# Order of the weight loads, of two norms and of the first projections at the start of an attention and gated-unit kernel

## The chip, the cores and the metric

The kernel runs on one core of a Trainium2 chip. The time is device microseconds of one execution; the text quotes medians of several executions. A profile is one execution taken by the hardware profiler, and its span (first to last instruction) is about 2 us shorter than the time. The engines are TensorE (PE in the profile; PEld is its weight load), VectorE (DVE), ScalarE (ACT), GpSimd (POOL) and SyncE (SP). SP and ACT also issue the loads. PEclk is the granted TensorE clock.

Some executions take 2 to 4 us longer, with a mean granted clock of 0.994 or less instead of 0.996 to 1.000. The ratios and intervals below count most of them as fast runs, because they lie within 1.5% of the fastest. Beside each ratio I therefore give the difference of the medians of the runs at a mean clock of 0.996 or more, called "full-clock runs". The kernel before differed from itself by 0.22 us in that measure; a smaller difference is not resolved here.

## The reference, cut to what matters

```python
B, S, D, F = 1, 2048, 512, 1792          # bfloat16
xn = layernorm(x)                        # no gain or bias, eps 1e-5
def A(xn):                               # sliding-window attention
    q, k, v = split_heads(xn @ wqkv)     # 32 heads of 16; wqkv is 512 x 1536: queries, keys, values
    p = softmax(mask(q @ k.T / 4))       # causal, window 256
    return (p @ v) @ wo
def B(xn):                               # gated unit without an activation
    return ((xn @ w_gate) * (xn @ w_up)) @ w_down
out = x + A(xn) + B(xn)
```

The change is aimed at the first 21 us. In that time the kernel loads x and the weights, normalises the first 512 rows of x (four blocks of 128 rows), transposes them on TensorE, and computes their queries, keys and values.

## The kernel before

The program is static, but its order is not written by hand. While the kernel is built, a small list scheduler works through the operations with assumed durations and assumed landing times of the loads, and emits each instruction to its engine in the order that this gives. On the chip the engines took their lists in this order, each instruction waiting for its data. The numbers `land`, `wkv` and `wq` are such assumptions: they change no wait, only the order. Below, values 0, keys 0 and queries 0 are the projections of block 0 of x; Wv, Wk and Wq are the three thirds of Wqkv; a load has landed when its last byte is there; and an apply is the instruction that normalises a block. The mode switches of the prediction are changes between groups of matmuls (dense, values, scores), for which the scheduler assumes a cost.

```python
def prologue(self):
    load(nc.sync,   self.x[0:64, 0, :],   xv[0:64, 0, :])        # block 0, two halves on two queues
    load(nc.scalar, self.x[64:128, 0, :], xv[64:128, 0, :])
    load(nc.scalar, self.x[:, 1, :],      xv[:, 1, :])           # block 1
    for k, cols in ((0, slice(512, 1536)), (2, slice(512, 1536))):   # keys AND values, in two halves
        load(nc.sync, self.Wqkv[:, k:k + 2, cols], w["qkv"][:, k:k + 2, cols])   # of the contraction
    load(nc.sync, self.x[:, 2, :], xv[:, 2, :])
    load(nc.sync, self.Wqkv[:, :, 0:512], w["qkv"][:, :, 0:512]) # queries
    load(nc.sync, self.x[:, 3, :], xv[:, 3, :])
    # ... cut: gate, up, down and output weights, the rest of x, constants
    self.keep_busy(42, 0)                # matmuls on ones, to warm up TensorE

def first_chunk(self):
    land = (3.6, 3.9, 7.3, 8.8)          # assumed landing of the four blocks of x
    wkv, wq = 6.3, 8.4                   # assumed landing of the weights
    applied, roots = [], []
    for b in range(4):
        # ... cut: bn = bn_stats + bn_aggr on DVE
        s = self.op(f"st{b}", {"V": ...}, [land[b]] + applied * (b == 1), bn, rank=0.5)
        s = self.op(f"sq{b}", {"A": ...}, [s], ...)     # sqrt(var + eps) on ACT
        s = self.op(f"rs{b}", {"V": ...}, [s], ...)     # reciprocal on DVE
        # ... cut: ap{b} on DVE, (x - mean) * rs; block 0 in two halves
        if b == 0:
            applied = [self.at_["ap", 0, 1]]            # block 1's statistics wait for block 0's apply
    for b in range(4):
        # ... cut: turn{b}: 4 transposes on PE, then a copy PSUM -> xnT by ACT or DVE
        self.add_v(0, b, wkv - 0.6)                                  # 16 matmuls each
        self.add(f"k0b{b}", 4.2, [("xnT", 0, b), wkv], ..., k_out)   # inner loop over k = 0..3
        self.add(f"q0b{b}", 4.2, [("xnT", 0, b), wq], ..., q_out)

def add_v(self, T, b, land=0.0):         # values: OUTER loop over k, so half the weights do half the work
    def emit(i):
        for k in range(4):
            for jj in range(2):
                # ... cut: 2 matmuls, lhsT = xnT[:, k, 64 tokens], rhs = Wqkv[:, k, 1024:1536]
```

The softmax here doesn't subtract the row's maximum and nothing guards it: scores larger than these inputs give would overflow.

## Time and profile before

| | before |
|---|---|
| time, median of 5 runs | 267.28 us (267.13 to 267.55) |
| time and span of the profiled run | 267.0 us, 265.0 us |
| PE busy | 259.0 us, 98% of the span |
| first value projection starts | 6.03 us |
| PE without a gap from | 9.46 us |

The chain of work that ended last, in order of time, starts like this (start us, length us, what; L148 is the loading helper, L205 the dense matmuls, L679 the value projections, L614 the transposes, L213 the scores):

```profile
3.32 6.10 DMA Wqkv<-in_A_wqkv_dram
9.41 0.05 issue
9.46 2.85 PE M L205 x48
...
20.03 0.33 PE S L213 x8
20.36 0.99 PE M L679 x16
```

After that the chain stays on PE until 258.9 us. So the kernel is bound by PE from 9.46 us on, and by loads before. The busy time by stretch, kernel before (each group: busy us and number of instructions; then PEclk, DMA share, GB/s):

```profile
5.00:9.46 4.46, 3.24 (x45) 2.40 (x45) 3.13 (x9) 2.04 (x6) 0.00 (x0) 1.00 1.04 366
9.46:20.00 10.54, 10.54 (x164) 9.11 (x168) 9.64 (x20) 4.51 (x8) 3.07 (x12) 1.00 1.07 378
20.00:260.00 240.00, 240.00 (x3202) 115.12 (x3202) 173.47 (x329) 156.62 (x106) 115.75 (x251) 1.00 0.11 29
```

From 9.46 to 260 us PE is busy all the time (10.54 of 10.54, 240.00 of 240.00); only the first line has something to win. What happens in it, from the timeline of the kernel before (start us, length us, engine, line, operation, out<-in, shapes, count, and in brackets the idle time before it and what ended that):

```profile
3.39 0.69 DVE L584 BATCH_NORM_STATS2 st<-x 128x6 f32<-128x512 bf16 x1 [1.46 <-DMA x<-in_A_x_dram]
4.86 0.60 DVE L271 TENSOR_SCALAR xn<-x,mv,rs 128x256 bf16<-128x256 bf16 x2
5.27 0.54 PE L614 MATMUL M<-ident,xn 128*128 128x128 bf16 x4 [0.63 <-DVE xn L271]
5.38 0.69 DVE L584 BATCH_NORM_STATS2 st<-x 128x6 f32<-128x512 bf16 x1
6.03 0.63 PE L679 MATMUL M<-Wqkv,xnT 128*64 128x256 bf16 x8
7.37 0.63 PE L679 MATMUL M<-Wqkv,xnT 128*64 128x256 bf16 x8 [0.71 <-DMA Wqkv<-in_A_wqkv_dram]
7.93 1.07 PE L205 MATMUL M<-xnT,Wqkv 128*128 128x128 bf16 x16
8.84 0.39 PE L614 MATMUL M<-ident,xn 128*128 128x128 bf16 x4
9.46 2.85 PE L205 MATMUL M<-xnT,Wqkv 128*128 128x128 bf16 x48 [0.24 <-DMA Wqkv<-in_A_wqkv_dram]
```

Values 0 stop half-way for the second half of the key and value weights (7.37). Then come keys 0 and the transposes of block 1, and then PE waits for the query weights (9.46).

### The profile page before, as it was taken

The numbers are of one execution on the slowest core, as the hardware profiler recorded it, in microseconds if no ns is written. First come the engines' busy times: TensorE is split into PE (matmuls) and PEld (weight loads), VectorE is DVE, ScalarE is ACT, GpSimd is POOL, SyncE is SP. The second block draws the span as 40 slices with busy tenths as digits, with TensorE's granted clock in tenths as the row PEclk, the third lists the DMA queues.
The fourth block names the chain that finished last, engine by engine and source line by source line (L and its number), as shares of the span: only waits on it lengthen the run. The fifth ranks groups of instructions, "written<-read, shape, count | busy, mean of one in ns | idle before, by whom it ended". The sixth has DMA issues, their size and how long they took to land.

```text
span 265.0 us, 8000 instructions
## 1 busy us (share of the span) xinstructions
PE 259.0 (98%) x3456; PEld 131.1 (49%) x3456; DVE 189.7 (72%) x367; ACT 165.0 (62%) x122; POOL 119.9 (45%) x272
## 2 busy tenths in 40 slices
PE   7899999999999999999999999999999999999994
PEld 6784444554435444465534454446545444544562
DVE  4889987888997628787997629796754449787404
ACT  4536676667767766777767676667886776673000
POOL 1223765654357372808256463708164545537000
PEclk9999999999999999999999999999999999999999
DMA  6999920000000400000001400000000000000002
GB/s 201 378 377 349 205 43 0 4 0 2 4 2 20 101 22 24 0 2 2 2 0 42 82 21 22 0 6 0 2 2 22 20 24 22 0 2 0 2 2 80
DMA packets 16739, 13.88 MB, mean 52 GB/s; under 512 B 7104, under 2 KB 16192, under 8 KB 16704
## 3 DMA queue, kind: packets, MB, share of 16 engines
q1 hardware_dynamic: 16336, 13.11, 16.5%
q8 instruction: 27, 0.44, 0.7%
q10 hardware_dynamic: 368, 0.26, 0.4%
q14 instruction: 8, 0.07, 0.1%
HBM read 9.70 MB, written 2.10 MB: 45 GB/s over the span
## 4 chain that ended last, share of the span: by engine, by line
PE 94%; DMA 3%; SPq 1%; DVE 1%; issue 0%
PE M L205 72%; PE S L213 9%; PE M L243 7%; PE M L679 5%; DMA Wqkv<-in_A_wqkv_dram 2%; SPq L148 1%; DMA out_dram<-xn 1%; PE S L205 1%; DVE xn L773 1%; PE M L614 0%
## 5 line engine op out<-in xcount | busy, mean ns | idle before, releaser
L495 ACT ACTIVATE P<-S 128x2048 bf16<-128x2048 f32 x76 | 140.9, 1854 | 55.2 <-PE S L213 51.7
L222 POOL TENSOR_SCALAR_AFFINE_SELECT P<-P 64x256 bf16<-64x256 bf16 (+1 forms) x248 | 112.8, 457 | 112.9 <-ACT P L495 100.8
L205 PE MATMUL M<-xnT,Wg 128*128 128x512 bf16 x224 | 57.7, 380 | 0.0
L205 PE MATMUL M<-xnT,Wu 128*128 128x512 bf16 x224 | 57.7, 380 | 0.0
L205 PE MATMUL M<-Wd,hT 128*128 128x512 bf16 (+1 forms) x224 | 52.1, 373 | 0.0
L731 DVE TENSOR_TENSOR hT<-M,gsb 128x512 bf16<-128x512 f32 x56 | 38.0, 678 | 7.6 <-PE M L205 7.3
L205 PEld LDWEIGHTS <-hT 128*128 128x128 bf16 x238 | 21.7, 98 | 23.5 <-issue 2.1
L205 PEld LDWEIGHTS <-Wu 128*128 128x128 bf16 x224 | 20.5, 98 | 25.1 <-issue 2.3
L205 PEld LDWEIGHTS <-Wg 128*128 128x128 bf16 x224 | 20.2, 98 | 24.5 <-issue 2.8
L201 DVE CAST gsb<-M 128x512 bf16<-128x512 f32 x40 | 27.4, 684 | 4.9 <-PE M L205 4.6
L205 PE MATMUL M<-xnT,Wqkv 128*128 128x128 bf16 (+1 forms) x224 | 30.4, 288 | 0.2 <-DMA Wqkv<-in_A_wqkv_dram 0.2
L531 DVE STREAM_TRANSPOSE at<-M 128x512 f32<-128x512 f32 x32 | 21.4, 698 | 12.3 <-PE M L243 12.3
L213 PE MATMUL S<-Q,K 32*128 32x320 bf16 (+3 forms) x720 | 30.0, 254 | 0.0
L228 DVE TENSOR_TENSOR P<-P,masks 128x512 int16<-128x512 int16 x56 | 22.5, 409 | 9.2 <-ACT P L495 9.2
L213 PEld LDWEIGHTS <-K 32*128 32x128 bf16 x720 | 11.9, 92 | 32.3 <-issue 31.3
L282 DVE TENSOR_SCALAR K<-M,own 128x512 bf16<-128x512 f32 x28 | 20.0, 743 | 3.7 <-PE M L205 3.4
L205 PEld LDWEIGHTS <-Wqkv 128*128 128x128 bf16 x224 | 15.8, 98 | 11.1 <-issue 1.4
L243 PE MATMUL M<-P,V 64*17 64x320 bf16 (+4 forms) x1440 | 19.5, 252 | 0.0
L773 DVE TENSOR_TENSOR y<-M,x 128x512 bf16<-128x512 f32 x12 | 8.2, 682 | 14.6 <-PE M L205 14.6
L243 PEld LDWEIGHTS <-V 64*17 64x17 bf16 x1440 | 17.1, 86 | 2.8 <-issue 0.8
L679 PE MATMUL M<-Wqkv,xnT 128*64 128x256 bf16 x256 | 15.9, 274 | 0.7 <-DMA Wqkv<-in_A_wqkv_dram 0.7
L205 PE MATMUL M<-Wo,OT 128*128 128x512 bf16 (+1 forms) x64 | 16.2, 374 | 0.0
(51 smaller groups left out, 134.0 us busy)
## 6 DMA issues: line engine op xcount, KB each, us to landing
Wg<-in_B_w_gate_dram SPq DMA_DIRECT2D x2, 896.0 KB, 10.3
Wu<-in_B_w_up_dram SPq DMA_DIRECT2D x2, 896.0 KB, 12.1
Wqkv<-in_A_wqkv_dram SPq DMA_DIRECT2D x3, 512.0 KB, 5.0
out_dram<-y SPq DMA_DIRECT2D x12, 128.0 KB, 1.7
x<-in_A_x_dram SPq DMA_DIRECT2D x1, 1024.0 KB, 14.1
Wd<-in_B_w_down_dram SPq DMA_DIRECT2D x2, 512.0 KB, 12.4
Wd<-in_B_w_down_dram SPq DMA_DIRECT2D x2, 384.0 KB, 8.5
x<-in_A_x_dram SPq DMA_DIRECT2D x1, 512.0 KB, 11.6
```

The costliest lines, as they stand in the source:

```text
L201: self.nc.vector.tensor_copy(out=out, in_=in_)
L205: self.nc.tensor.matmul(ps, lhsT=a, rhs=b, start=first and n == 0, stop=last and n == len(pairs) - 1)
L213: self.nc.tensor.matmul(self.S[:, e, 64 * at:64 * (at + m)], lhsT=self.K[U % 3][rows, c, j].rearrange("p l t -> p (l t)"), rhs=self.Q[T % ...
L222: self.nc.gpsimd.affine_select(out=v, in_=v, pattern=[[0, 4], [0, n], [sign, 64]], base=0, fill=0.0, compare_op=ALU.is_gt if kind else ALU ...
L228: self.nc.vector.tensor_tensor(out=v, in0=v, in1=m, op=ALU.bitwise_and)
L243: self.nc.tensor.matmul(banks[lane][32 * e:32 * e + 17, 64 * q:64 * (q + m)], lhsT=self.V[U % 3][rows, j, 4 * c + e, 0:17], rhs=P[rows, e, ...
L282: self.nc.vector.tensor_scalar(out=out, in0=in_, scalar1=own, scalar2=None, op0=ALU.mult)
L495: ex = self.op(f"exp{g}", {"A": (took + 0.06, took + 0.18)}, [o], lambda e: self.nc.scalar.activation(out=P[:, :, 0:hi], in_=self.S[:, :, ...
L531: t = self.op(f"tr{v}", {"V": (0.63, 0.71)}, [o] + ts, lambda e, par=par: nc.vector.transpose(out=self.at[:, :, par, :], in_=self.M[banks[ ...
L679: self.nc.tensor.matmul(self.M[i][64 * lane:64 * lane + 64, 256 * jj:256 * jj + 256], lhsT=self.xnT[T % 2][:, k, tok], rhs=w[:, lane], sta ...
L731: x = self.op(f"u{T}.{f}", {"V": PSUM_COPY["V"]}, [o, ("gate", T, f)], lambda e: self.nc.vector.tensor_tensor(out=self.hT[T % 2][:, f, :], ...
L773: self.nc.vector.tensor_tensor(out=keep["y"][:, cols], in0=self.M[i][:, cols], in1=self.x[:, t, cols], op=ALU.add)
```

## The change

Its intent is to let PE start on values as soon as a third of the weights is there, and to have two blocks ready by then: load values, keys and queries one by one; compute the statistics of block 1 right after those of block 0; tell the scheduler landing times that put both value projections ahead of the keys.

```diff
-        for k, cols in ((0, slice(512, 1536)), (2, slice(512, 1536))):
-            load(nc.sync, self.Wqkv[:, k:k + 2, cols], w["qkv"][:, k:k + 2, cols])
-        load(nc.sync, self.x[:, 2, :], xv[:, 2, :])
-        load(nc.sync, self.Wqkv[:, :, 0:512], w["qkv"][:, :, 0:512])
-        load(nc.sync, self.x[:, 3, :], xv[:, 3, :])
+        for n, lo in enumerate((1024, 512, 0)):
+            load(nc.sync, self.Wqkv[:, :, lo:lo + 512], w["qkv"][:, :, lo:lo + 512])
+            if n:
+                load(nc.sync, self.x[:, n + 1, :], xv[:, n + 1, :])
...
-        land = (3.6, 3.9, 7.3, 8.8)
-        wkv, wq = 6.3, 8.4
+        land = (3.4, 3.9, 8.0, 9.9)
+        wv, wk, wq = 6.2, 7.7, 9.6
...
-            s = self.op(f"st{b}", {"V": (0.92, 0.94)}, [land[b]] + applied * (b == 1), bn, rank=0.5)
+            s = self.op(f"st{b}", {"V": (0.92, 0.94)}, [land[b]], bn, rank=0.5)
...
-            self.add_v(0, b, wkv - 0.6)
-            self.add(f"k0b{b}", 4.2, [("xnT", 0, b), wkv], lambda i, f=project: f(i, 512), k_out)
+            self.add_v(0, b, wv)
+            self.add(f"k0b{b}", 4.2, [("xnT", 0, b), wk], lambda i, f=project: f(i, 512), k_out)
```

The built order on PE becomes: transposes 0, four warming matmuls, transposes 1, values 0, values 1, keys 0, queries 0, transposes 2, keys 1, queries 1, transposes 3, and so on, with values 2 and 3 after the first scores. Before, it was: transposes 0, values 0, keys 0, transposes 1, queries 0, keys 1, queries 1.

More of the change, by code (lines that the diff above doesn't have):

```diff
@@ L573, in first_chunk @@
     def first_chunk(self):
-        land = (3.6, 3.9, 7.3, 8.8)
-        wkv, wq = 6.3, 8.4
+        land = (3.4, 3.9, 8.0, 9.9)
+        wv, wk, wq = 6.2, 7.7, 9.6
         nc = self.nc
-        applied, roots = [], []
+        roots = []
         for b in range(4):
@@ L597, in first_chunk @@
                 self.at_["ap", b, n] = self.op(f"ap{b}", {"V": took}, [s], lambda e, b=b, cols=cols: self.i_apply(b, cols), rank=0)
-            if b == 0:
-                applied = [self.at_["ap", 0, 1]]
         self.op("table", {"A": (1.5, 1.5)}, roots + [("Q", 0, 0, 2)], lambda e: nc.scalar.activation(
```

## The prediction

> **What bounds the kernel now.** TensorE. The page shows PE busy 259.0 us of a 265.0 us span (98%) at a granted clock of 1.0; the chain of waits is 94% PE. Read in order of time, that chain starts with the third Wqkv load (3.32 to 9.41 us), and from 9.46 us runs without a break on PE to 258.9 us. The change moves work but removes none, so it can gain only what PE loses before 9.46 us, plus mode switches.
>
> **The start, from the timeline.** Warm-up matmuls end at 4.64. The first norm (statistics at 3.39, apply at 4.86) lets the transposes start at 5.27 and the first value projection at 6.03. It stops half-way, for 0.71 us, for the second Wqkv half (landed 7.33). Keys run 7.93 to 9.00, transpose 1 at 8.84, then PE waits for Wq (landed 9.41).
>
> **What the change does.** Loads: the same bytes in the same places, so I expect Wv near 5.8, Wk near 7.3, Wq near 9.4 us. Rows of Wv and Wk shrink from 2048 to 1024 B; packets of 1024 B take about 45 ns, of 2048 B 81 to 93 ns: the same rate, which agrees with the Trainium skill, "DMA: Bandwidth & Descriptors", Specifications (line rate from 512 B).
> DVE: statistics of block 1 (x landed 3.75) run directly after those of block 0, so apply 0 starts at about 5.40 instead of 4.86; apply 1 ends near 6.6 instead of 7.26.
> PE order, from the built program: transposes 0, four fillers, transposes 1, values 0 and 1, keys 0, queries 0, transposes 2, keys and queries 1, transposes 3, four projections, first gate and up, first scores, then values 2 and 3 together (before: 1 and 2 together, 0 and 3 alone).
>
> **Sum (estimate from these durations).** Transposes 0 start 5.4 + 0.41 = 5.8 and end 6.35; fillers to 6.74; transposes 1 to 7.13. Values 0 start at 7.1, over a microsecond later than before, but without a stop: values 0 and 1 take 1.87 us (32 matmuls in the chain) to 9.0. Keys 0 to 9.95, then queries 0, 0.5 us after Wq landed. No later wait should appear: apply 2 is ready at 10.5 against its use near 10.9, apply 3 at 12.6 against 13.2.
> From 7.13 the chain's durations give 13.8 us until all projections of block 0, first gate/up and first scores are done: 20.95 us. Before, that point is 21.35. Gain 0.4 us, of which 0.1 us is the pairing of the values (32 take 1.87, twice 16 take 1.98). Everything after is PE-bound and moves left by it; the built program has as many matmuls (3456) and 180 instead of 182 mode stretches.
>
> The clock should stay at 1.0: the longest PE gap is about 1.2 us; the Trainium skill, "TensorE: Matmul & The Clock Gate", Part 1, names some 3.4 us of idling.
>
> **Prediction.** 266.9 us, range 266.3 to 267.5. Faster by over 2%: 0.01; within 2%: 0.98; slower: 0.01.
>
> **What would show it.** Timeline: no DMA wait on PE after 5 us; values 0 start near 7.1; continuous PE from there; first scores near 19.1 instead of 19.96; last value projection ends near 21.0. The chain begins with x loads, DVE and PE rather than Wqkv.
>
> **What would make it wrong.** Wq later than 10 us; block 0's norm delayed over 0.6 us; evacuations (DVE holds apply 2 behind a value copy) stopping PE between 9 and 17 us; new small PE stalls later, since evacuations are reassigned between DVE and ACT.

## The result, and the profile after

| | before | after |
|---|---|---|
| time, median of 5 runs | 267.28 us (267.13 to 267.55) | 266.00 us (265.92 to 266.21) |
| time and span of the profiled run | 267.0 us, 265.0 us | 266.21 us, 264.4 us |
| first value projection starts | 6.03 us | 6.62 us |
| PE without a gap from | 9.46 us | 9.85 us, with three projections done instead of two |
| first scores and all value projections of the first 512 rows done | 21.35 us | 20.65 us |

The ratio is 0.9952, interval 0.9938 to 0.9967. A ratio here is the mean time of one kernel's fast runs over that of the other's of the same rounds, so it is not quite the ratio of the medians quoted. By the 2% measure the two are the same; the gain of 1.28 us is still well outside the scatter of this group, and outside the predicted range (266.3 to 267.5).

The same lines of the timeline, kernel after:

```profile
3.33 0.69 DVE L583 BATCH_NORM_STATS2 st<-x 128x6 f32<-128x512 bf16 x1 [1.39 <-DMA x<-in_A_x_dram]
4.16 0.66 DVE L583 BATCH_NORM_STATS2 st<-x 128x6 f32<-128x512 bf16 x1
5.12 0.60 DVE L270 TENSOR_SCALAR xn<-x,mv,rs 128x256 bf16<-128x256 bf16 x2
5.52 0.54 PE L611 MATMUL M<-ident,xn 128*128 128x128 bf16 x4 [0.41 <-DVE xn L270]
6.30 0.40 PE L611 MATMUL M<-ident,xn 128*128 128x128 bf16 x4
6.62 1.94 PE L676 MATMUL M<-Wqkv,xnT 128*64 128x256 bf16 x32
8.49 1.07 PE L204 MATMUL M<-xnT,Wqkv 128*128 128x128 bf16 x16
9.85 1.07 PE L204 MATMUL M<-xnT,Wqkv 128*128 128x128 bf16 x16 [0.29 <-DMA Wqkv<-in_A_wqkv_dram]
```

The apply of block 0 comes 0.26 us later than before (5.12 against 4.86), not 0.54 as I had it. Values 0 and 1 run as one unbroken stretch of 32 matmuls from 6.62. Keys 0 follow without a wait. Queries 0 still wait, 0.29 us, for the query weights. Those land later than before; the loads of Wqkv, before and after (count, size, median us from issue to landing):

```profile
Wqkv<-in_A_wqkv_dram SPq DMA_DIRECT2D x3, 512.0 KB, 5.0
```

```profile
Wqkv<-in_A_wqkv_dram SPq DMA_DIRECT2D x3, 512.0 KB, 5.6
```

The chain of the kernel after, in order of time:

```profile
3.42 6.39 DMA Wqkv<-in_A_wqkv_dram
9.81 0.05 issue
9.85 1.07 PE M L204 x16
...
18.45 0.33 PE S L212 x8
18.78 1.87 PE M L676 x32
```

So the chain still begins with the query weights, landing at 9.81 instead of 9.41 us. The gain is the third projection that PE has finished by then.

The two profiles differ by 0.59 us of span (264.97 and 264.39 unrounded), the medians by 1.28 us. The sum, from the traces: the start of the last value projection's last matmul moved from 21.08 to 20.38 (0.70 gained); from there to the last matmul the kernel after needs 240.22 us against 240.08 (0.13 lost, told below); the end is equal within 0.01. Outside the span, time minus span is 2.0 us before and 1.8 us after (0.2 gained). The traces show one thing there: behind the last instruction of all five profiles of the order of before, two packets move that the profile calls "instruction" (8 KB each, in the DMA view of the 4 us behind the span), the last of them 1.41 to 1.42 us behind it, once 1.69; in the order of after there are none. In two experiments told below the last one starts 1.32 us behind (e_norms, time minus span 1.93) and 1.13 us behind (e_wqlate, 1.75). Where such packets come, the time outside is longer the later the last one comes (r_before, with 1.69 and 2.00, is the exception); that they cause it was not tested. The rest, 0.49 us, is that the profiled run of before was faster than its five timed runs (267.0 against 267.28) and that of after the slowest of its five (266.21 against 266.00).

### The profile page after: what moved, and what is told of

Same layout as the page of the kernel before. It is cut to its first block, busy times and chain, and to the rows that moved or that the text cites. A ratio compares the mean times of both kernels' runs of the same rounds, so it can differ in the third digit from the quotient of the medians.

```text
span 264.4 us, 7996 instructions
## 1 busy us (share of the span) xinstructions
PE 259.3 (98%) x3456; PEld 131.7 (50%) x3456; DVE 187.2 (71%) x362; ACT 167.6 (63%) x127; POOL 119.9 (45%) x272
## 4 chain that ended last, share of the span: by engine, by line
PE 93%; DMA 3%; SPq 1%; ACT 1%; DVE 1%; issue 0%; ACTq 0%
PE M L204 71%; PE S L212 9%; PE M L242 7%; PE M L676 5%; DMA Wqkv<-in_A_wqkv_dram 2%; SPq L148 1%; ACT P L494 1%; DMA out_dram<-xn 1%; PE S L204 1%; DVE xn L770 1%; PE M L611 0%; ACTq L494 0%
## 5 line engine op out<-in xcount | busy, mean ns | idle before, releaser
L200 DVE CAST gsb<-M 128x512 bf16<-128x512 f32 x38 | 26.0, 683 | 5.8 <-PE M L204 5.7
L281 DVE TENSOR_SCALAR K<-M,own 128x512 bf16<-128x512 f32 x24 | 17.2, 742 | 2.3 <-PE M L204 2.1
L198 ACT ACTIVATE gsb<-M 128x512 bf16<-128x512 f32 x18 | 10.8, 598 | 9.0 <-PE M L204 9.0
```

The source lines that it names most:

```text
L200: self.nc.vector.tensor_copy(out=out, in_=in_)
L281: self.nc.vector.tensor_scalar(out=out, in0=in_, scalar1=own, scalar2=None, op0=ALU.mult)
```

## The experiments

Eighteen runs were made, in five groups, each on one chip and beside its own runs of the kernel before. All gave correct results.

### Repeats of both kernels

No edit. The question was whether the gain is fixed, or set in each run by the loads.

> The kernel before, unchanged, for a second profile and an A-A comparison. Theory A (the whole gain is PE idling saved in the first 21 us; I mis-sized the norm chain of block 0): ratio 1.000 within 0.1%; the point where first scores and the last value projection of block 0 are both done is again near 21.35 us in its trace. Theory B (the first profile of before was a lucky one, and typical runs start PE's unbroken stretch later, because the loads land later or the clock is released later): ratio again 1.000, but this profile shows that point 0.3 us or more later, with the Wq load landing at 9.7 or later.

> The changed kernel, unchanged, for a second profile. Ratio 0.995 (about 1.3 us less). Theory A: first scores and value projections 2 and 3 done at 20.65 us again, and the Wq load lands after 9.8 us again, because its loads have 1024-byte rows. Theory B: that point lies at 20.3 us or earlier, with Wq landing near 9.4, since the first profile was of the slowest of the five runs.

> The changed kernel once more, for a third profile and five more times; two earlier groups gave medians 266.0 (all within 0.3) and 266.9 (266.19 to 270.75). Theory A (a fixed gain): 266.0 to 266.3 again, ratio 0.995. Theory C (the start of the unbroken PE stretch is set in each run by when block 1 of x and Wq land; the floor is 264.1 us of span): the spans of the runs lie between 264.1 and 265.6, and in the profile the span is 244.0 us plus the start of the 64th value-projection matmul of the first chunk, whatever that is.

> The changed kernel a fourth time, as the yardstick of this group. Ratio 0.995 to 0.9985, as its groups so far.

> The changed kernel as the yardstick for the version with both additions on the same chip: 0.5 to 1.0 us faster than before, in the profile a wait of queries 0 for Wq of 0.3 to 0.4 us if Wq lands after 9.8.

| run | median (range), us | ratio to before (interval) | full-clock medians: this, before, difference |
|---|---|---|---|
| first group | 266.00 (265.92 to 266.21) | 0.9952 (0.9938 to 0.9967) | 266.00, 267.28, -1.28 |
| r_before | 267.03 (266.76 to 268.99) | 1.0009 (0.9986 to 1.0032) | 266.94, 267.16, -0.22 |
| r_after | 266.90 (266.19 to 270.75) | 0.9985 (0.9971 to 0.9999) | 266.68, 267.16, -0.48 |
| r_after2 | 266.41 (265.89 to 266.65) | 0.9941 (0.9905 to 0.9977) | 266.41, 267.23, -0.82 |
| r_after3 | 266.58 (266.27 to 266.84) | 0.9971 (0.9948 to 0.9994) | 266.58, 267.16, -0.58 |
| r_after4 | 266.43 (266.15 to 269.69) | 0.9996 (0.9957 to 1.0034) | 266.41, 267.02, -0.61 |

The gain of full-clock runs is 0.5 to 0.8 us in four groups and 1.28 in the first; the kernel after has full-clock medians of 266.4 to 266.7 in those four, inside the range that I predicted. So it is partly the draw of the first group that put the measured time outside that range. Theory A (a fixed gain) falls. Of theory C two parts hold. The spans of the full-clock runs lie between 264.1 and 265.6. And behind the last value projection every profile of one order takes the same time within 0.12 us (240.08 before, 240.22 to 240.33 after), whatever happened ahead of it.

What differs between runs is, first, when x and the weights land: in the full-clock profiles of the kernel after, values 0 start at 6.62 to 7.09 us and the wait for Wq is 0.29 to 0.40 us. A second thing differs, which the mean clock does not show: when the clock is first released. In the profiles where this falls into the warm-up, its matmuls start about 107 ns apart up to the first record of the full clock and 56 to 60 ns apart behind it. That record lies between 3.49 and 6.66 us in all profiles but one. In r_after4 (6.47) the apply of block 0 started at 5.10, as in the first profile (5.12), but from the first transpose to values 0 it took 1.24 us instead of 1.10. So a full-clock run can hide a late release.

The runs of 264.1 us of span are 0.3 us below the first profile, which is what that profile's wait for Wq would account for; no profile was taken of such a run, so this is argued and not shown. Theory B of r_before (a long stretch that starts later, Wq landing at 9.7 or later) failed: Wq landed at 9.20 and the stretch started at 9.24. Its point of first scores and value projections lies at 21.14, not at 21.35 again. The profile of r_after fell on a slow run and decides neither of its two theories.

### The loads alone, the order alone

e_loads and e_loads2 are the kernel before with the load lines of the diff only; the order on every compute engine is exactly that of before. e_oldloads and e_oldloads2 are the kernel after with those lines put back; every compute engine has exactly the order of after.

```diff
 e_loads, against before: only the loads of Wqkv, x block 2 and x block 3 as in the kernel after
 e_oldloads, against after: only these loads as in the kernel before
```

> Before with only the loads changed (values, keys, queries one by one); the instruction order of every compute engine is exactly that of before. Theory A: no gain, ratio 0.999 to 1.002: values 0 no longer stop half-way, but keys 0 then wait for Wk (7.3 to 8.0 us) and queries 0 for Wq (9.4 to 9.8 us), which still begins the unbroken stretch of PE. A rival (the loads themselves are the gain, the data arrive in the order of use): ratio 0.997 or less, unbroken stretch from before 9.3 us.

> The new loads with the order of before, again. If the new loads are a wash or a small loss by themselves: ratio to before 1.000 to 1.002, as in its first group (1.0013). If they gain by themselves: 0.998 or less.

> The changed kernel with only the loads put back as before (two halves of keys and values, then queries); the order on every compute engine is exactly that of the changed kernel. Theory A: most of the gain stays, ratio to before 0.995 to 0.997: values 0 start near 6.6, stop up to 0.6 us for the second half (7.3 us), keys 0 end near 9.7, queries 0 right after. The rival (the loads are the gain): ratio 0.999 or more.

> The changed order with the loads of before, again. If the new loads are a wash (they cure the stop inside values 0 but all landings come some 0.4 us later): within 0.3 us of the changed kernel of this group. If they carry a part of the gain where the chip's landings are favourable: 0.4 us or more slower than the changed kernel.

| run | median, us | ratio (interval) | full-clock difference to before |
|---|---|---|---|
| e_loads | 267.40 | 1.0013 (1.0001 to 1.0025) | +0.24 |
| e_loads2 | 267.48 | 1.0008 (0.9987 to 1.0028) | +0.32 |
| e_oldloads | 266.67 | 0.9994 (0.9967 to 1.0021) | -0.51 |
| e_oldloads2 | 266.51 | 0.9999 (0.9961 to 1.0037) | -0.72 |
| both changes, same two chips (r_after, r_after3) | 266.90 and 266.58 | 0.9985 and 0.9971 | -0.48 and -0.58 |

The two e_oldloads groups hold one and two slow-clock runs (269.12; 269.19 and 268.67), which is why their ratios say nothing; the other runs lie between 266.40 and 266.85. The order carries the gain. The loads by themselves lose a quarter of a microsecond, because PE then waits for each of the three. From the timeline of e_loads:

```profile
6.41 1.06 PE L678 MATMUL M<-Wqkv,xnT 128*64 128x256 bf16 x16 [0.36 <-DMA Wqkv<-in_A_wqkv_dram]
7.91 1.07 PE L204 MATMUL M<-xnT,Wqkv 128*128 128x128 bf16 x16 [0.43 <-DMA Wqkv<-in_A_wqkv_dram]
9.79 2.85 PE L204 MATMUL M<-xnT,Wqkv 128*128 128x128 bf16 x48 [0.59 <-DMA Wqkv<-in_A_wqkv_dram]
```

Under the new order the loads are a wash: full-clock medians of 266.68 with the new loads against 266.65 with the old ones on one chip, 266.58 against 266.43 on the other. They cure the stop inside values 0, and everything lands later: over the profiles with the loads of before the first part of Wqkv landed at 6.0 us on average (5.8 to 6.4) and Wq at 9.5 (six profiles each), with the new loads at 6.6 (6.0 to 7.0) and 9.9 (eight profiles).

### Which part of the order

```diff
 e_norms, against after
+            s = self.op(f"st{b}", ..., [land[b]] + applied * (b == 1), bn, rank=0.5)   # as before
 e_normsonly, against before
-            s = self.op(f"st{b}", ..., [land[b]] + applied * (b == 1), bn, rank=0.5)
+            s = self.op(f"st{b}", ..., [land[b]], bn, rank=0.5)                        # and land = (3.4, ...)
 e_wqlate, against before
-        wkv, wq = 6.3, 8.4
+        wkv, wq = 6.3, 9.6
 e_bsplit, against before
-        load(nc.sync, self.Wqkv[:, :, 0:512], w["qkv"][:, :, 0:512])
+        for at in (0, 256):
+            load(nc.sync, self.Wqkv[:, :, at:at + 256], w["qkv"][:, :, at:at + 256])
```

> The changed kernel with one part undone: the statistics of block 1 again follow the apply of block 0. The build then puts values 0 first, transposes 1 next, keys 0, queries 0 and keys 1, so values 1 no longer fills the wait for the weights. If the gain comes from filling PE with values 1 before Wk and Wq land: no gain is left, ratio to before 0.999 to 1.002, PE waits for Wk (to about 7.9) and for Wq (to 9.4 to 9.8). If the gain came from the loads or the later end of the schedule: ratio 0.997 or less.

> Before with the norms of blocks 0 and 1 side by side and the loads and assumed landings of the weights left; the build then puts transposes 1 ahead of keys 0, and values 0 and 1 behind keys 0. If the gain comes from having both blocks transposed before the second half of the weights lands, whichever projection is first: 0.1 to 0.5 us slower than the changed order with the loads of before, as keys 0 need both halves at once (7.3 to 7.9 us) where values 0 can do a half; still 0.2 us or more faster than before. If values ahead of keys is what matters: no gain over before.

> Before with one number changed, the assumed landing of Wq (8.4 to 9.6), which makes the build put keys 1 before queries 0. Transposes 1 stay behind keys 0. If it is enough to put other work before queries 0: the gain of the change, span 264.1 to 264.4. My theory says not enough, since block 1 is only transposed at 8.84 to 9.23 us and copied by ACT until 9.86, so keys 1 start at 9.9 where queries 0 started at 9.3 to 9.8: span 265.1 to 265.6, ratio 1.000 to 1.002.

> Before with Wq loaded in two column halves and nothing else; the order on every compute engine is that of before. If before is bound by the landing of Wq (queries 0 stand right behind keys 0 and transposes 1, done at 9.23 us): queries 0 start at 9.2 to 9.3 instead of 9.25 to 9.8, span 264.8 to 264.9 in all fast runs, ratio 0.998 to 0.999. If the start of the long stretch is set by something else: no change.

| run | PE order after transposes 0 | median, us | ratio (interval) | full-clock difference |
|---|---|---|---|---|
| e_norms | values 0, transposes 1, keys 0, keys 1, queries 0, queries 1 | 266.37 | 0.9944 (0.9909 to 0.9979) | -0.86 |
| e_normsonly | transposes 1, keys 0, values 0, values 1 | 267.32 | 1.0007 (0.9976 to 1.0038) | +0.03 |
| e_wqlate | values 0, keys 0, transposes 1, keys 1, queries 0 | 267.30 | 1.0014 (1.0001 to 1.0026) | +0.32 |
| e_bsplit | as before | 266.94 | 0.9995 (0.9983 to 1.0008) | -0.04 |

Three of the four expectations failed. I expected no gain from e_norms, and an order with queries 0 ahead of keys 1; the build put keys 1 first, and it gained 0.86 us (r_after2 on the same chip: 0.82). The rival named there, that the loads gain, is excluded by e_loads. Some of the gain does lie behind the start (from its last matmul to the end of the span e_norms takes 3.65 us, the other kernels of this section 3.78 or more), but the start alone is as good: the last value projection of the first 512 rows is done at 20.86 us, in r_after2 at 20.99. So the norms side by side, named in the change, are not needed. Its timeline shows why:

```profile
6.06 1.06 PE L678 MATMUL M<-Wqkv,xnT 128*64 128x256 bf16 x16
7.31 0.40 PE L613 MATMUL M<-ident,xn 128*128 128x128 bf16 x4 [0.18 <-DVE xn L270]
7.70 3.84 PE L204 MATMUL M<-xnT,Wqkv 128*128 128x128 bf16 x64
```

The transposes of block 1 now stand before keys 0, and the four projections from 7.70 run without a wait for Wq, which landed at 9.54: keys 1 fill the time. e_wqlate also puts keys 1 before queries 0, but leaves transposes 1 behind keys 0, and keys 1 then start at 10.29 after a wait of 0.69 us for the copied block 1: no gain, as expected. So it takes both: block 1 transposed early, and a third projection ahead of queries 0. (The two also differ in their loads, which gain nothing by themselves.) From the timeline of e_wqlate:

```profile
10.29 1.95 PE L205 MATMUL M<-xnT,Wqkv 128*128 128x128 bf16 x32 [0.69 <-ACT xnT L199]
```

e_normsonly has both blocks transposed by 6.6 us, but keys first. Its keys 0 loop over the whole contraction for each output, so they need both halves of the weights; PE did two matmuls and then waited 1.20 us, to 8.07. It gained nothing (its six runs scatter from 266.44 to 269.00):

```profile
6.59 0.28 PE L205 MATMUL M<-xnT,Wqkv 128*128 128x128 bf16 x2
8.07 0.95 PE L205 MATMUL M<-xnT,Wqkv 128*128 128x128 bf16 x14 [1.20 <-DMA Wqkv<-in_A_wqkv_dram]
```

With the loads of before it is therefore values first that matters, since values can do half their work with half the weights. I had expected at least 0.2 us from the transposes alone.

e_bsplit was to show that before is bound by the landing of Wq alone. In its profile queries 0 did start at 8.89, a span of 264.4. But the other four runs have spans of 264.9 to 265.1, as the kernel before (264.9 to 265.2 in all but two of its runs there), and the medians do not differ. The second half of the key and value weights is a bound close behind: in that profile queries 0 started 1.7 us of PE work after it had landed. Which of the two binds in the other runs I cannot say, as each submission has one profile; the idea that the wait for Wq alone holds before back is not supported.

### The two waits that are left in the kernel after

```diff
 e_x1first, against after
-        load(nc.scalar, self.x[:, 1, :], xv[:, 1, :])
+        load(nc.sync, self.x[:, 1, :], xv[:, 1, :])       # ahead of the weights
 e_wqsplit, against after: Wq in two column halves, as in e_bsplit
 e_best, e_best2: both of these
 e_x1late, against after: block 1 of x behind the value weights on the SP queue
```

> The changed kernel with block 1 of x loaded on the SP queue ahead of the weights instead of on the ACT queue; PE and DVE orders unchanged. If a late block 1 of x is what spreads the changed kernel's runs (its statistics now stand before the apply of block 0): block 1 lands by 3.9 us, values 0 start at 6.6 us or earlier, no run above 265.0 us of span. Wq then lands as before or up to 0.3 us later, so if the Wq wait is the cause instead, the spread stays (264.1 to 265.6).

> The changed kernel with Wq loaded in two column halves; every compute engine keeps the changed kernel's order. The first 256 columns should land some 0.6 us before the whole, so queries 0 need not wait at 9.56 us. If the wait for Wq is what spreads the changed kernel's runs: median span 264.1 to 264.3, no DMA wait on PE. If not (the spread comes from block 1 of x and the norms): median as the changed kernel's within 0.1 us.

> The changed kernel with block 1 of x loaded late on purpose (behind Wv on the SP queue, landing near 6.9 us instead of 3.75 to 4.25). If the norms side by side make block 0 wait for block 1: transposes 0 start near 8.3 us, values 0 near 9.2 to 9.7, PE idle for some 3 us from 4.7 to 5.5 on; the time grows by at least 2.3 us, and by up to 4.5 us if the granted clock falls to half meanwhile, as it did in the one slow profile (7.0 to 13.9 us). If block 0 does not depend on block 1: within 0.5 us of the changed kernel.

> The changed kernel with both additions: block 1 of x on the SP queue ahead of the weights, Wq in two column halves; PE and DVE orders unchanged. If the two waits left in the changed kernel are the late block 1 and Wq: no DMA wait on PE after 5 us, values 0 start at 6.6 to 6.8, then unbroken, the 64th value projection of the first chunk at 20.1 to 20.3, span 263.9 to 264.2 in all runs; ratio 0.993 or less, a little better than either addition alone (266.16 and 266.3 us).

> The changed kernel with block 1 of x ahead of the weights and Wq in halves, beside the changed kernel on one chip. If the two waits (late block 1, late Wq) are what the changed kernel still loses: 0.2 to 0.4 us faster than the changed kernel, no run above 266.5 us. If not: within 0.1 us of it.

| run | median (range), us | ratio to before (interval) | kernel after on the same chip |
|---|---|---|---|
| e_x1first | 266.16 (265.85 to 266.51) | 0.9936 (0.9901 to 0.9971) | 266.41 |
| e_wqsplit | 266.30 (265.98 to 266.50) | 0.9938 (0.9899 to 0.9976) | 266.41 |
| e_best | 266.14 (265.58 to 266.27) | 0.9961 (0.9947 to 0.9974) | not run there |
| e_best2 | 265.83 (265.63 to 267.40) | 0.9959 (0.9940 to 0.9978) | 266.43 |
| e_x1late | 269.54 (269.34 to 270.64) | 1.0108 (1.0087 to 1.0130) | not run there |

Alone, Wq in halves gained 0.11 us on the kernel after, which is not resolved, and block 1 first 0.25, hardly more than the resolution. In e_wqsplit's profile the wait for Wq was gone, as expected, but its median span was 264.5, not the 264.1 to 264.3 of that expectation; so the wait for Wq is not what spreads the runs. e_x1first kept a wait for Wq (0.41 us in its profile) and spread as the kernel after did there (spans of 264.0 to 264.7 against 264.1 to 264.8). e_best missed its ratio (0.9961 instead of 0.993 or less) and its span (263.8 to 264.4 instead of 263.9 to 264.2), and its profile still has a wait of 0.19 us, for the second half of Wq. e_best2 gained more than the 0.2 to 0.4 us expected, and had one run above the 266.5 us expected as its limit: both additions together were 0.6 us faster than the kernel after on that chip and 1.2 us faster than before (0.8 for e_best on the other chip). Five of the six runs of e_best2 took 265.63 to 265.93, below every run of the kernel after in that group (266.15 and up). So this version beats both kernels, with one run of 267.40, told below.

That the two waits are what it removes is not shown: nearly all of the gain lies behind the start, as told at the end of this section. The two waits have a different weight. Queries 0 wait some 0.3 us. A late block 1 is worse, since with the norms side by side its statistics stand in DVE's list before the reciprocal and the apply of block 0, and block 0 waits with it. One profile of e_oldloads2 fell on such a run. Its timeline, DVE then PE:

```profile
5.96 0.69 DVE L584 BATCH_NORM_STATS2 st<-x 128x6 f32<-128x512 bf16 x1 [1.60 <-DMA x<-in_A_x_dram]
6.95 0.60 DVE L271 TENSOR_SCALAR xn<-x,mv,rs 128x256 bf16<-128x256 bf16 x2
```

```profile
7.35 0.54 PE L612 MATMUL M<-ident,xn 128*128 128x128 bf16 x4 [2.23 <-DVE xn L271]
8.67 3.24 PE L677 MATMUL M<-Wqkv,xnT 128*64 128x256 bf16 x32
```

Block 1 landed at 5.94 us instead of 3.8, block 0's apply came at 6.95 instead of 5.12, and PE stood idle for 2.23 us. Then the clock fell. The stretches of the same profile (PEclk is the third number from the end):

```profile
4.56:7.97 3.41, 1.18 (x17) 0.84 (x15) 1.91 (x7) 0.72 (x4) 0.00 (x0) 1.00 1.06 384
7.98:11.38 3.40, 3.40 (x33) 2.63 (x32) 1.63 (x5) 1.10 (x4) 2.39 (x11) 0.50 1.07 376
```

For 3.41 us the granted clock was 0.50, and the 32 value matmuls took 3.24 us instead of 1.94. This run took 269.19 us at a mean clock of 0.994. In r_after's profile block 1 landed at 6.59, the clock was 0.50 for 6.83 us and the run took 270.75. e_x1late makes it happen on purpose: block 1 landed at 6.62, transposes 0 started at 8.04 after 2.76 us of idling, the clock fell to 0.50 for 3.41 us in the profile, and all four runs took 269.34 or more with mean clocks of 0.994 to 0.987. The cause of the two profiled slow runs in the order of the kernel after is therefore shown; its other slow runs (269.12, 268.67 and 269.69 us) have no profile, and theirs may be another. In the order of before, block 1 late costs nothing on its path: in the profile of e_bsplit it landed at 5.71, and transposes 0 started at 5.29 as ever. Before has slow runs at 0.994 as well (five of the 54 runs that stood beside the experiments), but no profile fell on one, and their cause stays open. Whether the change makes slow runs rarer is not decided by so few.

The 267.40 run of e_best2 was the profiled one. Block 1 landed at 4.86 there, and the clock record begins at full rate only at 10.1 us; values 0 and 1 took 3.10 us instead of 1.94:

```profile
7.71 3.10 PE L678 MATMUL M<-Wqkv,xnT 128*64 128x256 bf16 x32
```

So block 1 can be late also from the head of the SP queue. More of the loss is the clock: the apply of block 0 came 0.77 us later than in e_best's profile, and values 0 and 1 alone took 1.16 us longer. The mean clock of this run is given as 1.0.

Nearly all of what e_best gains on the kernel after lies elsewhere. From the last value projection of the first 512 rows to the last matmul its two profiles, and those of e_x1first and e_x1late, take 240.07 to 240.08 us, though PE and DVE have the order of the kernel after; that kernel takes 240.22 or more. From the start of the last matmul to the end of the span, where little but the last stores is left, e_best and e_best2 take 3.36 and 3.35 us, e_x1first and e_x1late 3.57, the kernel after 3.79 to 3.81. For e_best the two make 0.57 us or more, as much as the whole difference of 0.6 us on the chip where both ran. At the start its profile is not resolved from the kernel after (last value projection's last matmul at 20.32 against 20.38 to 20.90). All four have one load less in the list of ACT. Comparing the traces matmul by matmul, of the first part, 0.13 us go at one place, where an exponential starts 0.78 us behind its scores in the kernel after and 0.51 us behind them in e_x1first; the chain names "issue", that is, nothing that the profile shows. The line in the timelines of the kernel after and of e_x1first (scores at 204.57 and 204.75):

```profile
205.35 1.88 ACT L494 ACTIVATE P<-S 128x2048 bf16<-128x2048 f32 x1 [1.33 <-PE S L212]
```

```profile
205.26 1.88 ACT L494 ACTIVATE P<-S 128x2048 bf16<-128x2048 f32 x1 [1.05 <-PE S L212]
```

This is the later loss to which the prediction gave no size, though it named small later stalls as a risk. Why ACT starts late there, and why the close is shorter in e_best, was not tested.

## Why the prediction was wrong

The direction and the place held: the gain inside the span is idle time of PE at the start. The size did not: 0.4 us forecast, 1.28 measured in the first group and 0.5 to 0.8 in four others. The step that failed is the sum for the start. "Values 0 start at 7.1" was 0.5 us too late (6.62 in the profile), and "No later wait should appear" left out 0.29 us of waiting for Wq. Two more terms were missing: 0.2 us outside the span, and a loss of 0.13 us or more late in the kernel.

The two errors at the start have opposite signs. Over all full-clock profiles (two of before, four of after) the last value projection's last matmul starts at 20.98 us on average before and at 20.62 after, 0.35 us earlier. That this lies near the 0.4 forecast is partly luck.

- "It can gain only what PE loses before 9.46 us, plus mode switches": right inside the span (mode switches were not measured by themselves). Behind the last value projection the traces differ by 0.13 us, and to the other side. But 0.2 us of the gain lies outside the profiled span (time minus span is 2.0 us in every run of the order of before and 1.8 in every run of the order of after). The instruction packets told with the result are a clue; the cause is not shown.
- "I expect Wv near 5.8, Wk near 7.3, Wq near 9.4 us": wrong. In the first profile they landed at 6.48, 7.95 and 9.81. The rate of the packets in steady state was right (1024 B in 46 ns, worked out for 16 engines 356 GB/s; the second 512 KB of Wqkv landed 1.5 us behind the first on average with either row size), and the Trainium skill, "DMA: Bandwidth & Descriptors", Specifications, agrees on that for rows of 1024 B. What I left out is the beginning: the first part of Wqkv, also 512 KB, landed at 6.55 us on average with 1024-byte rows and at 6.02 with 2048-byte rows, and everything behind it shifted. The traces show where: up to 4.0 us about as many packets of these loads have started with either row size (53 to 103 of 2048 B in seven profiles, 54 to 100 of 1024 B in eight), so half as many bytes. Why the start goes by packets the runs do not show.
- "apply 0 starts at about 5.40": 5.12. I added whole durations. Consecutive DVE instructions overlap at their ends: the second statistics started at 4.16, 0.10 us after the aggregation before it had started, although that is listed with 0.18.
- "Values 0 start at 7.1": this is the step that failed most, by 0.5 us: 6.62 in the profile. 0.28 us of it is the apply, the rest is the same error on PE: I added the listed 0.54 and 0.39 us of the transposes and the fillers, but the last of four transposes listed with 0.54 starts 0.33 us behind the first; from the first transposes to the first value matmul it took 1.10 us, not 1.3.
- "then queries 0, 0.5 us after Wq landed" and "No later wait should appear": wrong. Values 0 were earlier and Wq later, so queries 0 waited 0.29 us. This gave back part of the 0.5 us. "The chain begins with x loads, DVE and PE rather than Wqkv" fell with it.
- "Values 0 and 1 take 1.87 us": right (6.62 to 8.49). The work behind 7.13, put at 13.8 us, measured 13.74 without the wait (20.65 less 6.62 less 0.29). First scores: 18.4 against "near 19.1"; last value projection 20.65 against "near 21.0".
- "Before, that point is 21.35": right for the profile, but I took one profile for the kernel. That run was 0.28 us faster than the median.
- "The clock should stay at 1.0": right in the usual run. I looked at the longest gap of a usual run and did not ask what a late block 1 would do, although the change put block 0 behind it.

In one sum, for the first group: 0.70 us gained at the start in the profiles where 0.40 was forecast, 0.13 lost later, 0.2 gained outside the span, 0.49 from where the two profiled runs stand among their runs.

And the reasons given for the change were only partly its causes: the norms side by side are not needed for the gain, the separate loads are a wash, and what counts is that block 1 is transposed early and that a third projection stands before the one whose weights come last.

## What to carry to other kernels

When an engine works through a fixed list at the start of a program, put work whose data are already there in front of the instruction that waits for the last load; the kernel with one more projection of 0.95 us there was 0.5 to 0.8 us faster in four groups, with some 0.35 us of it at the start by the profiles. Compare the traces behind the changed place too: what e_best gained lay there. Before an early load is put in the path of another block, ask what a late landing of it would cost, since here that was 2 us and a halved clock. For changes under 1%, one profile is one draw of the landing times: read several, and estimate a chain by start-to-start times, since listed durations of pipelined instructions don't add.

## What the Trainium skill lacked or had wrong

- "TensorE: Matmul & The Clock Gate", Part 1, says the clock is released around 4 us into sustained matmul activity, give or take 0.5 us. Here the scatter is wider. The matmuls began at 0.83 or 0.84 us, and the record of the full clock begins between 3.49 us (the first profile of before) and 6.66 us in nineteen of twenty profiles, that is 2.7 to 5.8 us into the activity, and at 10.1 us in one (e_best2), in which PE was busy for 6.33 of the 7.13 us from 3.00 to 10.13. The mean granted clock of that run is still given as 1.0, so it does not show a late release.
- The same part gives the cold state as following at least one idle window of some 3.4 us. The length agrees (3.41 us at half clock, once 6.83). But the window before need not be idle: the clock fell after windows in which PE was busy 1.18 of 3.41 us (e_oldloads2) and 1.08 of 3.41 (r_after), and held after 2.19 of 3.41 (e_wqlate, 4.59 to 8.00).
- "DMA: Bandwidth & Descriptors", Specifications, gives 512 B as enough for line rate. Query weights in rows of 512 B took 27 to 32 ns a packet in the median (256 to 303 GB/s over 16 engines, worked out), in rows of 1024 B 46 ns (356 GB/s) and of 2048 B 84 ns (390 GB/s).
- I found no page that says that the row size matters at the start of a program when the rate behind it is about the same (the second 512 KB landed 1.5 us behind the first with either row size): the first 512 KB landed 0.5 us later on average in rows of 1024 B (6.0 to 7.0 us) than of 2048 B (5.8 to 6.4), with about as many packets started by 4.0 us.
- I found no page that gives the scatter of a small early load: 128 KB on the ACT queue, issued behind 64 KB, landed between 3.7 and 6.6 us in the profiles.
- I found no page that says that the time outside the profiled span depends on the program (it would belong to "Runtime: NRT & Kernel Launch"): here it was 2.0 us in the order of before and 1.8 us in the order of after, in every run, 1.9 in e_norms and 1.7 in e_wqlate.
